# Reordering the first loads of a fused attention and gated-unit kernel: projection rows first, the first tile in halves on a second queue

## The chip, the cores and the metric

One core of a Trainium2 chip runs the whole program. The metric is device microseconds of one execution. The kernel before took 264.89 us, the median of three runs (264.78, 264.89, 264.89).

## The reference, cut to what matters

The input x has 2048 rows of 640 columns in bf16. It is normalised row by row, and the normalised rows feed two branches whose results are added to x:

```
xn  = (x - mean) / sqrt(var + 1e-5)                      # per row, no gain or bias
q, k, v = split(xn @ wqkv)                               # 640 -> 3 x 640, 32 heads of 20
A   = softmax(q . k[s - 2w], w = 0..7, masked) @ v[...]  # 8 keys per position, 2 apart
A   = A @ wo
B   = ((xn @ w_gate) * (xn @ w_up)) @ w_down             # 640 -> 1536 -> 640
out = x + A + B
```

Every product after the first step needs xn transposed (columns on partitions), so nothing of the real matrix work can start before one tile of 128 rows is loaded, normalised and transposed.

## The kernel before, in words

The work on x goes by 16 tiles of 128 rows (t = 0 to 15); the projections and the gated unit go by four blocks of 512 rows. Columns are handled in five chunks of 128, since a matmul contracts over 128 partitions.

An order is planned at build time by a small list scheduler in the kernel (class Sched). Each engine's work is yielded as tasks, with an estimated ready time; the scheduler keeps a clock for every engine (`K.t`) and emits the task that its estimates let start first, by priority. `land=` gives the scheduler the time at which a load is expected to land, and `occ=` the time that an operation is expected to take. These numbers only order the instructions: on the chip every engine runs its own list in that order, and semaphores make it wait for what it reads.

Per tile, `front(t)` makes this chain: the load of x (`x_load`, a DMA of 160 KB); two statistics instructions of 320 columns each on VectorE (L577); their aggregate (L580); a square root on ScalarE (L587); a reciprocal (L594); the normalisation into XNS on VectorE (L606 for tiles 0 and 1, in two parts of 256 and 384 columns; L609 for tiles 2 to 5); five transposes on TensorE (L645, `trans`) into PSUM for tiles 0 to 3; and copies from PSUM into XNT (ScalarE L658, VectorE L656 and L665). From tile 4 on the transpose is a DMA issued by SyncE (L678).

`proj_group` makes the Q and K products. For tiles 0 and 1 (`spread`, L733) the contraction is cut into steps given by `STEPS`, chunks 0 and 1, then 2, then 3 and 4, so that a step can start when its chunks are there. Q and K of tiles 0 and 1 are 100 matmuls of 128 columns. Later tiles use L701. The weights WQKV come by `wqkv_load(g, lo, hi)`: g = 0 is Q, 1 is K, 2 is V, and lo to hi are the chunks (rows of the weight matrix, 160 KB per chunk).

Before the first transposes TensorE has no data; `warm` gives it matmuls on constants (L685): ten of 512 columns from the start, and three of 256 columns behind tile 0's transposes.

All loads of the first stage go through SyncE's queue, in this order: x tile 0; Q chunks 0 to 2 (480 KB); x tile 1; K chunks 0 to 2 (480 KB); Q chunks 3 and 4 (320 KB); x tile 2; K chunks 3 and 4 (320 KB); x tiles 3 to 11; V (800 KB); x tiles 12 to 15, each of which waits for its buffer. ScalarE's queue carries one small read named `touch` (5 KB: 64 bytes from every eighth row of the Q columns, into a buffer TCH that nothing reads), issued at the same time as tile 0. ScalarE then loads its activation table (1.28 us) before its first square root.

The main part that follows is a stream of matmuls: projections (L701), logits (L1016), gate and up (L1318), the sums of the weighted values (L1254), down and output projection (L1419, L1470), while VectorE and GpSimd make the products of attention.

Of the kernel before, what the change touches and what calls it, by code (L numbers as in the profile page):

```python
# [11 lines left out]
NCH = 5  # L12
# [9 lines left out]
TS = 128  # L22
# [335 lines left out]
def build_kernel(nc, A_x, A_wqkv, A_wo, B_x, B_w_gate, B_w_up, B_w_down, out):  # L358
# [5 lines left out]
    def sb(name, shape, dtype=BF16, at=None):  # L364
        n = mybir.dt.size(dtype)
        for s in shape[1:]:
            n *= s
        n = (n + 63) // 64 * 64
        if at is None:
            at = place[0]  # L370
            place[0] += n
        assert at + n <= 229344, (name, at + n)
        return K.sbuf(name, shape, dtype, at)
# [65 lines left out]
    MV = sb("MV", [128, NT, 2], FP32)  # L439
    SD = sb("SD", [128, NT, 4], FP32)  # L440
    DUM = sb("DUM", [128, 16], FP32)
    TCH = sb("TCH", [128, NCH, 32])
    ZERO = sb("ZERO", [128, JB])
    UF = [sb("UF0", [128, JB], at=a_xr + 4 * D * 2), ZERO]
    EPSC = sb("EPSC", [128, 16], FP32)
# [17 lines left out]
    def mark(*k):  # L463
        done.add(k)
# [38 lines left out]

    PARTS = (((0, 2), (2, NCH)), ((0, 2), (2, NCH)))
    COPY = (("act", "act"), ("dve", "act"))
    STEPS = (((0, 2), (2, 3), (3, NCH)), ((0, 2), (2, 3), (3, NCH)))

    def part_of(t, c):
        return next(k for k, (lo, hi) in enumerate(PARTS[t]) if lo <= c < hi)

    def xslot(t):
        return t + 4 if t < 8 else t - 8

    def x_load(t, eng="sp", land=None):
        dma(XST[:, xslot(t), :], xhbm[t * TS:(t + 1) * TS, :], w=[XST[:, xslot(t), :]], name=f"xld{t}", eng=eng, land=land)
        mark("x", t)

    wqkv_src = A_wqkv.rearrange("(c p) n -> p c n", p=128)

# [49 lines left out]
    def front(t):  # L569
        x, st = XST[:, xslot(t), :], STATS[:, t, 0:12]  # L570
        xs, mv = XNS[:, t % NXN, :], MV[:, t, 0:2]
        sd, rstd, nmr = SD[:, t, 0:1], SD[:, t, 1:2], SD[:, t, 2:3]
        p = 0.1 * t

        def stats(i):
            o, a = st[:, 6 * i:6 * i + 6], x[:, i * DHALF:(i + 1) * DHALF]
            op("dve", lambda e: e.bn_stats(o, a), r=[a], w=[("st", t, i)], name=f"bn{t}_{i}", occ=0.49)  # L577

        def aggr():
            op("dve", lambda e: e.bn_aggr(mv, st), r=[("st", t, 0), ("st", t, 1)], w=[("mv", t)], name=f"bnag{t}", occ=0.2)  # L580

        ts = next((g for g in GROUPS if t in g), (t,))
        t0, t1 = ts[0], ts[-1] + 1

        def sqrt():
            o, i = SD[:, t0:t1, 0:1], MV[:, t0:t1, 1:2]
            op("act", lambda e: e.activation(o, i, ACT.Sqrt, bias=EPSC[:, 0:1]), r=[("mv", k) for k in ts] + [EPSC[:]],  # L587
               w=[("sd", k) for k in ts], name=f"sd{t}", occ=0.36)
            for k in ts:
                mark("sd", k)  # L590

        def recip():
            o, i = SD[:, t0:t1, 1:2], SD[:, t0:t1, 0:1]
            op("dve", lambda e: e.reciprocal(o, i), r=[("sd", k) for k in ts], w=[("rstd", k) for k in ts], name=f"rstd{t}", occ=0.16)  # L594
            if t >= N_DVE_A:
                n, m = SD[:, t0:t1, 2:3], MV[:, t0:t1, 0:1]
                op("dve", lambda e: e.scalar_tensor_tensor(n, m, -1.0, o, op0=ALU.mult, op1=ALU.mult),
                   r=[x for k in ts for x in (("mv", k), ("rstd", k))], w=[("nmr", k) for k in ts], name=f"nmr{t}", occ=0.13)
            for k in ts:
                mark("rstd", k)  # L600

        def apply():
            if t < N_SPLIT:
                for a, b in [(128 * lo, 128 * hi) for lo, hi in PARTS[t]]:
                    o, i = XNS[:, t, a:b], x[:, a:b]
                    op("dve", (lambda o, i: lambda e: e.tensor_scalar(o, i, mv[:, 0:1], rstd, op0=ALU.subtract, op1=ALU.mult))(o, i),  # L606
                       r=[i, ("mv", t), ("rstd", t)], w=[o], name=f"lnap{t}", occ=0.09 + (b - a) * 0.55e-3)
            elif t < N_DVE_A:
                op("dve", lambda e: e.tensor_scalar(xs, x, mv[:, 0:1], rstd, op0=ALU.subtract, op1=ALU.mult),  # L609
                   r=[x, ("mv", t), ("rstd", t)], w=[xs], name=f"lnap{t}", occ=0.45)  # L610
            else:
                op("act", lambda e: e.activation(xs, x, ACT.Identity, bias=nmr, scale=rstd),
                   r=[x, ("nmr", t), ("rstd", t)], w=[xs], name=f"lnap{t}", occ=0.75)
            mark("apply", t)

        yield have("x", t)
        if t == 1:
            yield have("apply", 0)
        for i in range(2):
            if t == 2 and i == 0:  # L620
                yield have("apply", 1)
            if t == 2 and i == 1:
                yield have("xnt", t - 1)
            if t in BN_AFTER and i == 1:
                yield have("rstd", t - 1)
            yield Task("dve", lambda: stats(i), r=[x], prio=p)
        yield Task("dve", aggr, r=[("st", t, 1)], prio=p)
        mark("mv", t)
        if t == ts[-1]:
            yield Task("act", sqrt, r=[("mv", t)], prio=p - 1)  # L630
            yield Task("dve", recip, r=[("sd", t)], prio=p)
        yield have("rstd", t)
        if t >= NXN:
            yield have("xnt", t - NXN)
        yield Task("dve" if t < N_DVE_A else "act", apply, r=[("rstd", t), x], w=[xs], prio=p)
        o = XNT[:, :, t * TS:(t + 1) * TS]
        if t < N_PE_T:
            hold = []

            def trans(*bs):  # L640
                tpvs = [PS[:, b, :].bitcast(BF16)[:, 0:NCH * 128].rearrange("p (c f) -> p c f", c=NCH) for b in bs]
                b, tpv = bs[0], tpvs[0]
                for c in range(NCH):
                    i, q = xs[:, c * 128:(c + 1) * 128], tpvs[part_of(t, c) if len(bs) > 1 else 0][:, c, :]
                    op("pe", (lambda q, i: lambda e: e.transpose(q, i, IDENT[:]))(q, i), r=[i, IDENT[:]], w=[q],  # L645
                       name=f"tr{t}_{c}", occ=0.057, lat=0.2)
                hold.extend(zip(bs, tpvs))
                if t == 0:
                    warm(3)

            def part(k, eng):
                b, tpv = hold[k]
                lo, hi = PARTS[t][k]
                a, i = o[:, lo:hi], tpv[:, lo:hi]
                if eng == "dve":
                    X = op("dve", lambda e: e.tensor_copy(a, i), r=[PS[:, b, :]], w=[a], name=f"xntcp{t}_0", occ=0.1 + 0.08 * (hi - lo))  # L656
                else:
                    X = op("act", lambda e: e.activation(a, i, ACT.Copy), r=[PS[:, b, :]], w=[a], name=f"xntcp{t}_1",  # L658
                           occ=0.12 + 0.12 * (hi - lo))
                K.free_bank(b, X)  # L660

            def copy():
                b, tpv = hold[0]
                if t < N_DVE_C:
                    X = op("dve", lambda e: e.tensor_copy(o, tpv), r=[tpv], w=[o], name=f"xntcp{t}", occ=0.49)  # L665
                else:
                    X = op("act", lambda e: e.activation(o, tpv, ACT.Copy), r=[tpv], w=[o], name=f"xntcp{t}", occ=0.75)
                K.free_bank(b, X)

            yield Task("pe", trans, r=[xs], prio=p, banks=len(PARTS[t]) if t < N_SPLIT else 1)  # L670
            if t < N_SPLIT:
                for k, e in enumerate(COPY[t]):
                    yield Task(e, (lambda k, e: lambda: part(k, e))(k, e), r=[PS[:, hold[k][0], :]], prio=p - 1)
            else:
                yield Task("dve" if t < N_DVE_C else "act", copy, r=[PS[:, hold[0][0], :]], prio=p)
        else:
            def dmat():
                op("sp", lambda e: e.dma_start_transpose(o, xs), r=[xs], w=[o], dma=True, name=f"dtr{t}", nbytes=200e3, occ=1.25, extra=1.3)  # L678

            yield Task("sp", dmat, r=[xs], prio=1)  # L680
        mark("xnt", t)
# [830 lines left out]
    N_DVE_A = 6  # L1512
    N_DVE_C = 5
    N_SPLIT = 2
    FIRST = 9
    GU_KEEP = 3
    HP_MAX = 0
# [3 lines left out]
    H_PRIO = 9  # L1521
    FIN_PRIO = 8

    x_load(0, land=3.2)
    tch = A_wqkv.rearrange("(c k p) n -> k c p n", k=16, c=NCH)[:, :, 0, 0:32]
    stores.append(dma(TCH[0:16], tch, w=[TCH[0:16]], name="touch", eng="act"))
    wqkv_load(0, 0, 3, land=5.1)
    x_load(1, land=5.5)
    wqkv_load(1, 0, 3, land=7.1)
    wqkv_load(0, 3, NCH, land=8.0)  # L1530
    x_load(2, land=8.5)
    wqkv_load(1, 3, NCH, land=9.6)
    K.t["act"] = 2.1
    warm(10, JB)

    def misc():
        yield have("xnt", NT - 1)
# [61 lines left out]
```

## Time and profile before

| what | value |
|---|---|
| median of 3 runs | 264.89 us |
| profiled execution, whole | 265.17 us |
| its span, first to last instruction | 263.4 us |
| TensorE busy in the span | 259.6 us (99%) |
| VectorE / ScalarE / GpSimd busy | 219.1 / 112.8 / 160.5 us |
| mean DMA rate over the span | 151 GB/s |
| DMA rate from 3 to 12 us, in the views of that stretch | 347 to 365 GB/s |
| granted TensorE clock | 1.0 throughout |

The span is the time from the first to the last instruction of one profiled execution; 1.77 us of that execution lie around it. Times in the timeline are counted from the start of the span. A matmul's end is modelled (a 128-column one is given 219 ns, though the next one starts some 57 ns later), so the spacing of starts is what tells the rate.

### The profile page before, as it was taken

How to read it: one execution, taken by the hardware profiler on the slowest of the kernel's cores; microseconds unless marked ns; L12 is line 12 of the kernel's file. 1: busy time of each engine (PE TensorE's matmuls, PEld its weight loads, DVE VectorE, ACT ScalarE, POOL GpSimd, SP SyncE). 2: the span in 40 equal slices, each digit the busy share in tenths (PEclk: the TensorE clock that was granted, in tenths of full speed). 3: DMA queues.
4: the chain of work that ended last, by engine and by line, in shares of the span. 5: the costliest groups of instructions: out<-in, count | busy, mean ns of one | idle time of the engine just before them, and what ended most of it. 6: DMA issues, size and time to landing. Idle time of an engine off the chain costs nothing.

```text
span 263.4 us, 4101 instructions
## 1 busy us (share of the span) xinstructions
PE 259.6 (99%) x1587; PEld 136.0 (52%) x1587; DVE 219.1 (83%) x259; ACT 112.8 (43%) x198; POOL 160.5 (61%) x97
## 2 busy tenths in 40 slices
PE   8999999999999999999999999999999999999996
PEld 3996964544444444444444444444444444445675
DVE  4798899999898798868779999999989989995041
ACT  3569987556622221224257665541324116211300
POOL 3000000000599999999983455899979999999300
PEclk9999999999999999999999999999999999999999
DMA  6985679933379996650249702566669865821621
GB/s 220 368 210 105 124 159 388 355 152 100 119 147 193 234 217 115 121 100 1 65 118 311 174 6 51 133 137 175 142 179 185 207 141 141 142 60 36 91 66 50
DMA packets 47843, 39.78 MB, mean 151 GB/s; under 512 B 23856, under 2 KB 45488, under 8 KB 47792
## 3 DMA queue, kind: packets, MB, share of 16 engines
q1 hardware_dynamic: 44848, 33.29, 48.4%
q0 software_dynamic: 2736, 6.16, 13.8%
q8 instruction: 12, 0.20, 0.3%
q10 hardware_dynamic: 240, 0.07, 0.1%
q14 instruction: 7, 0.06, 0.1%
HBM read 25.07 MB, written 7.23 MB: 123 GB/s over the span
## 4 chain that ended last, share of the span: by engine, by line
PE 96%; DMA 2%; SPq 0%; DVE 0%; issue 0%
PE PS L1318 39%; PE PS L701 23%; PE PS L1419 21%; PE PS L1470 7%; PE PS L1016 2%; DMA WQKV<-in_A_wqkv_dram 2%; PE PS L733 2%; PE PS L1254 2%; SPq L482 0%; PE PS L645 0%; DVE FB L1483 0%
## 5 line engine op out<-in xcount | busy, mean ns | idle before, releaser
L1200 POOL TENSOR_TENSOR SV<-PV 128x1024 bf16<-128x1024 f32 x40 | 94.1, 2524 | 17.8 <-DVE SM L1049 4.2
L1195 DVE TENSOR_TENSOR PV<-VX,PS 128x1024 f32<-128x1024 bf16 (+1 forms) x54 | 90.7, 1730 | 2.8 <-POOL SV L1200 2.8
L701 PE MATMUL PS<-XNT,WQKV 128*128 128x512 bf16 (+2 forms) x390 | 60.7, 316 | 0.0
L1318 PE MATMUL PS<-XNT,WG 128*128 128x512 bf16 x240 | 59.7, 379 | 0.0
L1318 PE MATMUL PS<-XNT,WU 128*128 128x512 bf16 x240 | 59.6, 379 | 0.0
L701 PEld LDWEIGHTS PS<-XNT,WQKV 128*128 128x128 bf16 x390 | 37.8, 112 | 21.9 <-ACT LOG L1027 0.8
L933 DVE TENSOR_TENSOR PRF<-PS,KT 128x1024 f32<-128x1024 f32 x32 | 38.0, 1218 | 0.3 <-PE PS L701 0.3
L1318 PEld LDWEIGHTS PS<-XNT,WG 128*128 128x128 bf16 x240 | 23.3, 98 | 28.7 <-issue 0.4
L1318 PEld LDWEIGHTS PS<-XNT,WU 128*128 128x128 bf16 x240 | 23.5, 98 | 28.3
L959 POOL TENSOR_TENSOR PRF<-PRF,PRF 128x1024 f32<-128x1024 f32 x8 | 21.0, 2634 | 21.6 <-DVE LOG L1076 21.6
L706 ACT ACTIVATE HT<-PS 128x512 bf16<-128x512 f32 x24 | 14.4, 598 | 35.4 <-PE PS L1318 35.4
L1419 PE MATMUL PS<-HT,WD 128*128 128x512 bf16 x120 | 27.5, 379 | 0.0
L884 DVE TENSOR_TENSOR PRD<-QT,KT 128x2048 bf16<-128x2048 bf16 x24 | 27.5, 1220 | 0.0
L706 ACT ACTIVATE UX<-PS 128x512 bf16<-128x512 f32 x15 | 9.0, 597 | 41.6 <-PE PS L1419 41.6
L1035 POOL MEMSET LOG<- 32x6 bf16 (+6 forms) x7 | 0.4, 95 | 42.8 <-ACT LOG L1027 42.8
L992 POOL TENSOR_TENSOR PRD<-PRF,PRF 128x1024 bf16<-128x1024 f32 x8 | 20.6, 2633 | 0.1
L970 POOL TENSOR_TENSOR PRF<-PRF,PRD 128x1024 f32<-128x1024 f32 x8 | 19.7, 2563 | 0.0
L1419 PEld LDWEIGHTS PS<-HT,WD 128*128 128x128 bf16 x120 | 11.7, 98 | 14.3 <-ACT OT L1263 0.4
L1419 PE MATMUL PS<-OT,WO 128*128 128x512 bf16 x75 | 18.6, 379 | 0.0
L1327 DVE TENSOR_TENSOR HT<-HT,PS 128x512 bf16<-128x512 bf16 x18 | 12.3, 686 | 7.2 <-PE PS L1318 7.1
L1483 DVE TENSOR_TENSOR FB<-PS,XR 128x320 bf16<-128x320 f32 (+2 forms) x9 | 4.1, 454 | 16.2 <-PE PS L1470 15.3
L577 DVE BATCH_NORM_STATS2 STATS<-XST 128x6 f32<-128x320 bf16 x32 | 14.2, 467 | 2.3 <-DMA XST<-in_A_x_dram 2.1
(76 smaller groups left out, 247.2 us busy)
## 6 DMA issues: line engine op xcount, KB each, us to landing
VX<-v_scratch SPq DMA_DIRECT2D x80, 130.0 KB, 3.0
PRF<-PRF POOLq DMA_DIRECT2D x8, 512.0 KB, 5.4
XST<-in_A_x_dram SPq DMA_DIRECT2D x16, 160.0 KB, 5.2
v_scratch<-VST SPq DMA_DIRECT2D x4, 640.0 KB, 6.4
WG<-in_B_w_gate_dram SPq DMA_DIRECT2D x1, 1920.0 KB, 8.8
WU<-in_B_w_up_dram SPq DMA_DIRECT2D x1, 1920.0 KB, 12.4
out_dram<-in_A_x_dram SPq DMA_DIRECT2D x1, 1920.0 KB, 18.1
WD<-in_B_w_down_dram SPq DMA_DIRECT2D x1, 1920.0 KB, 8.4
```

What stands on the lines that cost most here:

```text
L701: op("pe", (lambda o, l, x, c, first: lambda e: e.matmul(o, l, x, start=first, stop=(c == NCH - 1)))(o, l, x, c, first), r=[l, x], w=[o], ...
L706: X = op("act", (lambda o, i: lambda e: e.activation(o, i, ACT.Copy))(o, i), r=[i], w=[o], name=name, occ=0.12 + n * 0.9e-3)
L884: op("dve", lambda e: e.tensor_tensor(s[:], qb, kv, ALU.mult), r=[q, rk], w=[s[:]], name=f"prod{j}_{r}_{c}", occ=1.15, lock=True)
L933: X = op("dve", lambda e: e.tensor_tensor(o[:], qb, kv, ALU.mult), r=[q, rk, ("qev", j, c)], w=[o[:]], name=f"prow{j}_{r}_{c}_{q0}", occ=1.17)
L959: yield Task("pool", lambda: op("pool", lambda e: e.tensor_tensor(x, x, y, ALU.add), r=[x, y] + tokens(), w=[x], name=name, occ=2.36, lock ...
L970: yield Task("pool", lambda: op("pool", lambda e: e.tensor_tensor(x, x, z, ALU.add), r=[x, z] + tokens(), w=[x], name=name + "c", occ=2.36 ...
L992: yield Task("pool", lambda: op("pool", lambda e: e.tensor_tensor(o, a, y, ALU.add), r=[a, y] + tokens(), w=[o], name=f"qend{j}_{r}_{q0}", ...
L1195: last[0] = op("dve", lambda e: e.tensor_tensor(p, vw, a, ALU.mult), r=[vv] + rk, w=[p], name=f"pv{u}_{x}_{r0}", occ=0.09 + 1.1 * nr)
L1200: X = op("pool", lambda e: e.tensor_tensor(o, p[:, :, 0, :], p[:, :, 1, :], ALU.add), r=[p[:]] + tokens(), w=[o], name=f"pva{u}_{x}", occ= ...
L1318: op("pe", (lambda l, x, c: lambda e: e.matmul(PS[:, b, :], l, x, start=(c == 0), stop=(c == NCH - 1)))(l, x, c), r=[l, x], w=[PS[:, b, :] ...
L1419: op("pe", (lambda l, x, i: lambda e: e.matmul(PS[:, b, :], l, x, start=(i == 0), stop=(i == n - 1)))(l, x, i), r=[l, x], w=[PS[:, b, :]], ...
L1470: op("pe", (lambda l, x, i: lambda e: e.matmul(dst, l, x, start=(i == 0), stop=(i == n - 1)))(l, x, i), r=[l, x], w=[PS[:, b, :]], name=f" ...
```

## The change

- Loads on SyncE's queue now run: Q chunks 0 to 2; K chunks 0 and 1 (320 KB); Q chunks 3 and 4; x tile 2; K chunks 2 to 4 (480 KB); x tiles 3 to 11 and so on as before.
- x tile 0 is issued on ScalarE's queue, as two DMAs of 320 columns each (80 KB, rows of 640 bytes); x tile 1 follows on the same queue. Each statistics instruction of tile 0 waits for its own half only.
- The read `touch` and its buffer go.
- The steps of tile 0's projection become chunks 0 and 1, then 2, then 3, then 4. The transposes of tiles 0 and 1 become two tasks each (two chunks, three chunks) with a PSUM bank each, where one task had made all five.
- One warming matmul fewer at the start (nine).
- The landing times given to the scheduler, and ScalarE's starting clock, are new.

In the resulting order of TensorE's instructions, the part up to tile 2's transposes reads as follows (number of matmuls; `tr` are transposes, `c` chunks):

```
before: 10 warm | tr0 5 | 3 warm | Q0 c0-2 15 | K0 c0-1 10 | tr1 5 | Q0 c3-4 10 | Q1 c0-1 10 | Q1 c2-4 15, K0 c2 5 | K0 c3-4 10 | tr2
after:   9 warm | tr0 5 | 3 warm | Q0 c0-2 15 | K0 c0-1 10 | tr1 2 | Q0 c3 5 | tr1 3 | Q0 c4 5 | Q1 c0-1 10 | Q1 c2-4 15 | K0 c2-3 10 | tr2
```

Further on, one group of five 512-column matmuls (a V projection of the first block) moves from before the first products of tiles 4 and 5 to just before the first logits. VectorE's order is unchanged. On ScalarE two more DMA issues stand ahead of the table load, and some evictions between about 40 and 70 us change places.

```diff
-    TCH = sb("TCH", [128, NCH, 32])
...
-    STEPS = (((0, 2), (2, 3), (3, NCH)), ((0, 2), (2, 3), (3, NCH)))
-
-    def part_of(t, c):
-        return next(k for k, (lo, hi) in enumerate(PARTS[t]) if lo <= c < hi)
+    STEPS = (((0, 2), (2, 3), (3, 4), (4, NCH)), ((0, 2), (2, 3), (3, NCH)))
...
+    def x_half(i, land, eng="sp"):
+        c = slice(i * DHALF, (i + 1) * DHALF)
+        dma(XST[:, xslot(0), c], xhbm[0:TS, c], w=[XST[:, xslot(0), c]], name=f"xld0_{i}", eng=eng, land=land)
+        if i:
+            mark("x", 0)
...
-            yield Task("dve", lambda: stats(i), r=[x], prio=p)
+            yield Task("dve", lambda: stats(i), r=[x[:, i * DHALF:(i + 1) * DHALF]] if t == 0 else [x], prio=p)
...
-            def trans(*bs):
-                tpvs = [PS[:, b, :].bitcast(BF16)[:, 0:NCH * 128].rearrange("p (c f) -> p c f", c=NCH) for b in bs]
-                b, tpv = bs[0], tpvs[0]
-                for c in range(NCH):
-                    i, q = xs[:, c * 128:(c + 1) * 128], tpvs[part_of(t, c) if len(bs) > 1 else 0][:, c, :]
+            def trans(k, *bs):
+                hold.extend((b, PS[:, b, :].bitcast(BF16)[:, 0:NCH * 128].rearrange("p (c f) -> p c f", c=NCH)) for b in bs)
+                for c in range(*PARTS[t][k]) if t < N_SPLIT else range(NCH):
+                    i, q = xs[:, c * 128:(c + 1) * 128], hold[k][1][:, c, :]
...
-                hold.extend(zip(bs, tpvs))
-                if t == 0:
-                    warm(3)
+                if t == 0 and k:
+                    warm(N_WARM)
...
-            yield Task("pe", trans, r=[xs], prio=p, banks=len(PARTS[t]) if t < N_SPLIT else 1)
             if t < N_SPLIT:
-                for k, e in enumerate(COPY[t]):
+                for k, ((lo, hi), e) in enumerate(zip(PARTS[t], COPY[t])):
+                    yield Task("pe", (lambda k: lambda *bs: trans(k, *bs))(k), r=[xs[:, lo * 128:hi * 128]], prio=p, banks=1)
                     yield Task(e, (lambda k, e: lambda: part(k, e))(k, e), r=[PS[:, hold[k][0], :]], prio=p - 1)
             else:
+                yield Task("pe", lambda b: trans(0, b), r=[xs], prio=p, banks=1)
...
+    N_WARM = 3
...
-    x_load(0, land=3.2)
-    tch = A_wqkv.rearrange("(c k p) n -> k c p n", k=16, c=NCH)[:, :, 0, 0:32]
-    stores.append(dma(TCH[0:16], tch, w=[TCH[0:16]], name="touch", eng="act"))
-    wqkv_load(0, 0, 3, land=5.1)
-    x_load(1, land=5.5)
-    wqkv_load(1, 0, 3, land=7.1)
-    wqkv_load(0, 3, NCH, land=8.0)
-    x_load(2, land=8.5)
-    wqkv_load(1, 3, NCH, land=9.6)
-    K.t["act"] = 2.1
-    warm(10, JB)
+    wqkv_load(0, 0, 3, land=4.8)
+    x_half(0, 2.8, "act")
+    x_half(1, 3.2, "act")
+    x_load(1, eng="act", land=4.2)
+    wqkv_load(1, 0, 2, land=5.9)
+    wqkv_load(0, 3, NCH, land=6.8)
+    x_load(2, land=7.3)
+    wqkv_load(1, 2, NCH, land=8.6)
+    K.t["act"] = 3.4
+    warm(9, JB)
```

## Prediction

> **What bounds the kernel now.** I read the chain of waits first. After one DMA that ends at 7.40 us it is TensorE to the last piece, without a gap:
>
> ```profile
> 2.26 5.14 DMA WQKV<-in_A_wqkv_dram
> 7.40 0.05 issue
> 7.45 0.75 PE PS L733 x10
> 8.20 0.28 PE PS L645 x5
> 8.48 2.86 PE PS L733 x50
> ...
> 14.41 29.39 PE PS L701 x235
> ...
> 261.16 0.02 issue
> 261.19 0.29 DVE FB L1483
> ```
>
> The work of TensorE is fixed, so the end moves by what its start and the stalls ahead of about 14 us move, unless a new stall opens. Next I read the timeline of the first 25 us (start, duration):
>
> ```profile
> 3.36 0.89 DVE L577 BATCH_NORM_STATS2 STATS<-XST 128x6 f32<-128x320 bf16 x2 [2.12 <-DMA XST<-in_A_x_dram]
> 6.26 1.00 PE L733 MATMUL PS<-XNT,WQKV 128*128 128x128 bf16 x15
> 7.45 0.75 PE L733 MATMUL PS<-XNT,WQKV 128*128 128x128 bf16 x10 [0.19 <-DMA WQKV<-in_A_wqkv_dram]
> ...
> 8.52 0.49 ACT L658 ACTIVATE XNT<-PS 128x384 bf16<-128x384 bf16 x1 [1.46 <-PE PS L645]
> 9.14 0.70 ACT L706 ACTIVATE QT<-PS 128x640 bf16<-128x640 f32 x1
> 9.95 0.30 ACT L587 ACTIVATE SD<-MV,EPSC 128x1 f32<-128x1 f32 x1
> 10.48 0.45 DVE L609 TENSOR_SCALAR XNS<-XST,MV,SD 128x640 bf16<-128x640 bf16 x1
> 11.18 0.44 PE L645 MATMUL PS<-IDENT,XNS 128*128 128x128 bf16 x5
> ```
>
> The statistics of tile 0 start when it has landed (3.33); from there to the first product (6.26) is one chain over VectorE, ScalarE and TensorE. The fifteen products start 57 ns apart (the chain has fifty in 2.86), so the last began at 7.06 and the next was due at 7.11. It came at 7.45: the modelled ends show a gap of 0.19, the starts one of 0.34.
>
> Then the DMA issues (KB each, us to landing) and the rates by stretch (last two columns: busy share of the DMA engines, GB/s):
>
> ```profile
> XST<-in_A_x_dram SPq DMA_DIRECT2D x1, 160.0 KB, 2.5
> TCH<-in_A_wqkv_dram ACTq DMA_DIRECT2D x1, 5.0 KB, 2.3
> ```
>
> ```profile
> 2.25:2.75 0.50, 0.50 (x3) 0.15 (x1) 0.00 (x0) 0.29 (x1) 0.28 (x2) 1.00 1.15 312
> 2.75:3.25 0.50, 0.50 (x2) 0.15 (x1) 0.00 (x0) 0.00 (x0) 0.28 (x3) 1.00 0.65 103
> 3.25:5.25 2.00, 1.76 (x5) 0.44 (x3) 1.46 (x5) 0.30 (x1) 0.51 (x3) 1.00 1.05 373
> ```
>
> Outside the hole from 2.75 to 3.25 the engines are full: bytes put ahead of a tile delay it by 160 KB per 0.45 us.
>
> **The change, part by part.**
>
> *Tile 0 in halves beside Q (the disputed term).* What counts is when the second statistics instruction starts: 3.36 + 0.445 = 3.81 before. Afterwards it is the later of the second half's landing + 0.03 and the first's + 0.48. A landing at 3.78 changes nothing. No row shows two queues sharing the engines on bulk loads. The early end is the nearest lighter row on that queue, a 64 KB store from ScalarE's queue late in the kernel, 1.6 us to landing: the halves, issued at 0.83 and about 1.25, would land at 2.43 and 2.85, a gain of 0.9. The late end has all 480 KB of Q served first: 3.33 + 1.33 = 4.66, a loss of 0.9. I take TCH, the row nearest in queue, place and moment: the first half lands at 0.83 + 2.3 = 3.13, the second 0.42 later, 3.55, since the hole has room for Q's bytes. The second statistics then start at 3.61: gain 0.20.
>
> *K chunks 0 and 1 as 320 KB, ahead of tile 2.* 1120 KB stand up to its end instead of 1280, 0.45 us less, so about 6.95 instead of 7.40, and the products need it at 7.06 - 0.20 + 0.05 = 6.9: the 0.34 go. Q chunks 3 and 4 (1440 KB instead of 1600) land near 7.85 where they landed at 8.3. Five transposes took 0.31 at 8.04 where the chain gives 0.28; that 0.03 goes too. Gain 0.37, or 0.3 if either is late by a tenth.
>
> *New order before tile 2's transposes: a new wait.* Counted with tile 0 unmoved: 6.26, 15 products to 7.10, 10 to 7.69, two transposes to 7.80, five products to 8.09, three transposes to 8.26, five products to 8.55, then 35 at 57 ns to 10.53. Tile 2 must be normalised by then. ScalarE's copy of the three chunks (0.49) can start at 8.46, the eviction of Q (0.70) behind it ends at 9.67, and the square root of tile 2 is queued behind both: 9.69 instead of 9.95. From there to the normalised tile took 0.98 (9.95 to 10.93), so it is ready at 10.67 and the transposes start at 10.72: TensorE waits 0.20. If tile 2 lands no earlier than 8.76 the wait is 0.45; with 0.45 us fewer bytes ahead I don't expect that. Everything behind on TensorE waits with it.
>
> *One V group moved back.* Five 512-column matmuls, 5 x 0.216 = 1.08 us, no longer stand before the products of tiles 4 and 5. Those began at 24.09 (two matmuls after 23.65 in this row), and need tile 5's transposing DMA:
>
> ```profile
> 19.43 1.27 SPq L678 DMA_TRANSPOSE XNT<-XNS  x1
> ```
>
> ```profile
> XNT<-XNS SPq DMA_TRANSPOSE x1, 3.7
> ```
>
> ```profile
> 23.65 0.92 PE L701 MATMUL PS<-XNT,WQKV 128*128 128x512 bf16 x5
> ```
>
> It lands at 23.13; TensorE now arrives at 23.01, and with 0.05 from landing to start waits 0.17 (0 if the first transpose, 2.29 us of issue at 17.09, shortens like its followers of 1.2 to 1.28; 0.6 if it doesn't follow TensorE's earlier start). The group is done later, in a stretch that stays full.
>
> *Parts that cost nothing.* One warming matmul less: TensorE stood idle from the end of the warming at about 5.0 to 5.45. Two more issues on ScalarE (0.45 each) put its table load (1.28) at about 2.15 to 3.45; the first square root was at 4.52, so 0.9 us cover it even with tile 0 earlier by 0.2. SyncE has two issues fewer ahead of tile 3; its queue is a backlog of bytes, so nothing moves. Dropping TCH frees 5 KB. The split of tile 0's transposes keeps their order.
>
> Sum: -0.20 - 0.37 + 0.20 + 0.17 = -0.20. The profiled execution took 265.17 (span 263.4), 0.28 above the median 264.89; set against the median, **264.7 us**.
>
> **The rivals.** 0.2%, 0.53 us, is about what a measurement tells from no change here.
>
> *Faster: the halves keep ahead of Q.* Were each half over as fast as its smaller size allows, at 2.8 and 3.2, the second statistics start at 3.28, gain 0.53; if one of the two new waits also fails to open, 0.53 + 0.37 - 0.2 = 0.70: 264.2 us. For it: the hole shows engines idle just there. Against it: TCH, 5 KB, needed 2.3.
>
> *The same, from packet for packet.* If the engines take one row of Q (1280 bytes) for each half row of tile 0 (640), 320 KB of Q go ahead of the second half: 3.33 + 0.9 = 4.23, loss 0.45, all else as above: 265.35, within 0.2%. The Trainium skill ("DMA: Bandwidth & Descriptors", Queues, rings and completion order) says that each engine takes turns between queues packet by packet, and that DMAs from different engines end up interleaved on the same 16; by that rule a second queue gives tile 0 no precedence. The trace of before bears on it only by TCH, whose packets ran in the same stretch as tile 0's.
>
> *Slower: Q first.* If Q's 480 KB, issued at the same moment and without the small read ahead of them, hold the engines, the second half lands at 4.66: loss 0.89, less the other terms' zero balance: 265.8 us. From a landing of 4.3 on it is slower by over 0.2%. For it: the hole is Q's own first packets being slow. Against it: it needs a whole queue to be passed over.
>
> *Slower: the changed order of Q chunk 3.* Three transposes of tile 1 now stand behind five products that wait for Q chunks 3 and 4. Should those land at 8.31 as before, the transposes move from 8.10 to 8.63 and all behind them by 0.53: 265.2; half a microsecond later still, 265.7.
>
> *Slower: the clock.* The warming matmuls start 0.43 apart until 4.22 and 0.40 apart after it, so the rate rises within the ninth, which is now the last. If it slipped to the end of an equally long busy stretch (3.75 us from 5.3), some forty matmuls would take 57 ns more: +2.3, 267. The Trainium skill ("TensorE: Matmul & The Clock Gate", Part 1) calls the window free-running and the moment variable from run to run; three runs within 0.11 us show none of that.
>
> **How the numbers follow.** My forecast 0.32, packet for packet 0.08, halves ahead 0.31, Q first 0.19, Q chunk 3 late 0.05, the clock 0.05. So faster 0.31, same 0.40, slower 0.29. The likeliest case alone: 264.4 to 265.1. The range reaches below the faster rival by 0.2 (both waits smaller) and to Q first: 264.0 to 265.8.
>
> **What would show it.** Right: statistics of tile 0 start separately near 3.2 and 3.6; the first L733 near 6.06; no DMA named before the K products; L645 of tile 2 waiting for XNS some 0.2; a DMA wait ahead of the first 256-column L701 of tiles 4 and 5. Wrong: a second statistics instruction before 3.3 or after 4.2, a wait for WQKV inside the first 40 products, or any TensorE idle beyond 25 us.

## The result: 1.2% slower

The changed kernel takes 267.99 us, the median of five runs (267.68 to 268.88), against 264.89 for the kernel before in the same comparison (264.78 to 264.98): a ratio of 1.0123, 95% interval 1.0112 to 1.0134. The forecast was 264.7 with a range of 264.0 to 265.8. The sign and the range were both wrong.

The profiled execution took 268.88 us with a span of 267.1 (before: 263.4), so it is 0.89 above its own median; its terms below are sized on it and are a little too large for the median. It also differs from the four others in its mean granted clock, listed as 1.000 where they have 0.994; the last section says what that means.

The chain of waits of the changed kernel (start, length, what) now hangs on tile 0's second half; `...` stands for lines left out:

```profile
0.83 0.43 ACTq L481
1.26 0.03 issue
1.29 4.13 DMA XST<-in_A_x_dram
5.42 0.02 issue
5.44 0.50 DVE STATS L579
...
7.14 0.79 PE PS L646 x5
7.93 0.64 PE PS L686 x3
8.57 2.67 PE PS L734 x25
11.23 0.21 PE PS L646 x2
11.45 0.53 PE PS L734 x5
11.98 0.32 PE PS L646 x3
12.30 2.44 PE PS L734 x40
14.74 0.28 PE PS L646 x5
...
18.09 29.39 PE PS L702 x235
```

The chain of before has, for tile 2's transposes and the 25 products behind them:

```profile
11.34 0.28 PE PS L645 x5
11.62 1.40 PE PS L733 x25
```

Three things are to be seen. The second half lands at 5.42 us, issued at 0.83 + 0.43. Tile 0's transposes start at 7.14, where they started at 5.45 before: 1.69 us. And 25 products take 2.67 us where 25 took 1.40 before. From there on nothing is new: the stream of 235 begins at 18.09 instead of 14.41 and takes 29.39 us in both, and the last piece of TensorE's work ends 3.7 us later as well.

The timeline has the two statistics instructions of tile 0 apart, as the change meant them to be, but late:

```profile
3.93 0.49 DVE L579 BATCH_NORM_STATS2 STATS<-XST 128x6 f32<-128x320 bf16 x1 [2.69 <-DMA XST<-in_A_x_dram]
5.44 0.49 DVE L579 BATCH_NORM_STATS2 STATS<-XST 128x6 f32<-128x320 bf16 x1 [1.02 <-DMA XST<-in_A_x_dram]
7.14 0.79 PE L646 MATMUL PS<-IDENT,XNS 128*128 128x128 bf16 x5 [2.28 <-DVE XNS L608]
7.72 0.85 PE L686 MATMUL PS<-const-bfloat16-1.0 128*128 128x256 bf16 x3
```

and before:

```profile
5.45 0.63 PE L645 MATMUL PS<-IDENT,XNS 128*128 128x128 bf16 x5 [0.45 <-DVE XNS L606]
5.92 0.50 PE L685 MATMUL PS<-const-bfloat16-1.0 128*128 128x256 bf16 x3
```

Before, the statistics ran back to back from 3.36, the second from 3.81. TensorE stood idle for 2.28 us ahead of the transposes, 0.45 before.

**Where the 3.7 us of span went.** 1.69 are the later transposes. From tile 0's transposes to those of tile 2 it was 5.89 us before (5.45 to 11.34 in the chain) and is 7.60 now (7.14 to 14.74), although five products fewer stand between them (5 x 57 ns = 0.28, which come behind instead: 3.35 from tile 2's transposes to the stream of 235, where it was 3.07). So for equal work this stretch costs 1.99 more. Rows of the chain account for it: the three warming matmuls take 0.64 where 0.33 is their length at full rate, the first 25 products 1.27 more, the rest up to 14.74 about 0.7 more, tile 0's five transposes 0.1 more (0.58 from their start to that of the warming matmuls behind them, 0.47 before); that is 2.4, and the 0.34 that TensorE waited for K's rows before is gone, which leaves 2.0.

The cause of the long products is the rate of TensorE, and the profile's page hides it. The busy time by stretch (PE busy and number of matmuls first, then the other engines; the last three columns are granted clock, DMA share and GB/s), before:

```profile
9.60:12.60 3.00, 3.00 (x58) 3.00 (x56) 2.20 (x8) 1.95 (x4) 0.00 (x0) 1.00 1.07 362
```

and after:

```profile
7.10:9.60 2.50, 2.46 (x20) 2.12 (x21) 2.07 (x7) 1.15 (x3) 0.00 (x0) 1.00 1.07 363
9.60:12.60 3.00, 3.00 (x31) 3.00 (x29) 1.08 (x4) 0.26 (x1) 0.00 (x0) 1.00 1.07 363
12.60:15.00 2.40, 2.40 (x46) 2.40 (x44) 1.22 (x4) 1.81 (x4) 0.00 (x0) 1.00 1.07 362
```

TensorE is fully busy in both, and the column of the granted clock says 1.00 in both, but it does 31 matmuls in the 3 us where it did 58. Only the count, or the spacing of starts (107 ns up to 12.5 us, 57 ns after 12.6), shows half rate. In the trace's own record the first stretch at full rate begins at 4.60 us before and at 12.61 us after.

### The profile page after: what moved, and what is told of

It is laid out like the page before. It is cut to its first block, busy times and chain, and to the rows that moved or that the text cites. A ratio compares the mean times of both kernels' runs of the same rounds, so it can differ in the third digit from the quotient of the medians.

```text
span 267.1 us, 4099 instructions
## 1 busy us (share of the span) xinstructions
PE 261.7 (98%) x1586; PEld 138.1 (52%) x1586; DVE 218.9 (82%) x259; ACT 112.6 (42%) x198; POOL 160.5 (60%) x97
## 4 chain that ended last, share of the span: by engine, by line
PE 96%; DMA 2%; DVE 1%; ACTq 0%; ACT 0%; issue 0%
PE PS L1319 39%; PE PS L702 22%; PE PS L1420 21%; PE PS L1471 7%; PE PS L734 3%; PE PS L1017 2%; PE PS L1255 2%; DMA XST<-in_A_x_dram 2%; PE PS L646 1%; PE PS L686 0%; DVE STATS L579 0%; ACTq L481 0%; DVE XNS L608 0%; ACT SD L589 0%; DVE FB L1484 0%
```

## The experiments

Twelve kernels were run, each beside the kernel before, whose median was 264.94 to 265.08 in these comparisons. In the code, too, `...` stands for lines left out. The theory after the result: the DMA engines served all of Q (480 KB) between tile 0's two halves, and the idle stretch that this made cost TensorE its rate.

**1. Why the second half came late.** Three edits of the changed kernel: all loads on SyncE's queue, with the halves ahead of Q (`one_queue`); Q's load cut in three (`q_chunks`); tile 0 as one load on ScalarE's queue, both statistics waiting for all of it (`x0_whole`).

```diff
 one_queue
-    wqkv_load(0, 0, 3, land=4.8)
-    x_half(0, 2.8, "act")
-    x_half(1, 3.2, "act")
-    x_load(1, eng="act", land=4.2)
+    x_half(0, 2.8)
+    x_half(1, 3.2)
+    wqkv_load(0, 0, 3, land=4.8)
+    x_load(1, land=4.2)
 q_chunks
-    wqkv_load(0, 0, 3, land=4.8)
+    for c in range(3):
+        wqkv_load(0, c, c + 1, land=4.8)
 x0_whole
-    x_half(0, 2.8, "act")
-    x_half(1, 3.2, "act")
+    x_load(0, eng="act", land=2.8)
...
-            yield Task("dve", lambda: stats(i), r=[x[:, i * DHALF:(i + 1) * DHALF]] if t == 0 else [x], prio=p)
+            yield Task("dve", lambda: stats(i), r=[x], prio=p)
```

> The changed kernel with every load on SyncE's queue, in the order: the two halves of tile 0, Q chunks 0 to 2, tile 1, K chunks 0 and 1, Q chunks 3 and 4, tile 2, K chunks 2 to 4. All instructions of the other engines are as in the changed kernel, nine warming matmuls too, and the touching read stays away. Theory (it is the second queue that makes the second half late): the halves land at 3.1 and 3.4, the second statistics start near 3.6, TensorE idles under 0.8 us and runs at full rate; 264.9 - 0.2 - 0.37 + 0.37 = 264.7 us (264.3 to 265.2). Rival (the loss comes from the missing touching read, from nine warming matmuls or from the new order of TensorE's instructions): 266 us or more.

> The changed kernel with Q chunks 0 to 2 loaded by three DMAs of 160 KB in a row where one of 480 KB stood; the halves of tile 0 stay on ScalarE's queue. Theory (the DMA engines take turns between the two queues by whole DMAs: first half, all of Q, second half, K, tile 1): now only 160 KB stand between the halves, 320 KB fewer, 0.9 us, so the second half lands at about 4.5 instead of 5.41, and the time falls by 0.9 if the half-rate stretch moves along: 267.1 us (266.3 to 267.5), 265 to 266 if the shorter idle time keeps the rate up. Rival (turns by rows or bytes, or the first queue simply has precedence): second half at 5.2 to 5.6, 267.7 to 268.9 us.

> The changed kernel with tile 0 as one DMA of 160 KB on ScalarE's queue instead of two halves; all else is unchanged. Theory (turns by whole DMAs): tile 0 is served whole in the first turn and lands at 3.9 + 0.45 = 4.3, both statistics run from there, so the second starts at 4.8 instead of 5.44: 0.65 us less, 267.3 us (266.6 to 267.7), less still if the rate rises earlier. Rival (turns by rows or bytes, or precedence of the first queue): the whole tile lands at about 5.4, the second statistics start at 5.9, 268.5 us (268.1 to 269.3).

Measured: `one_queue` 265.43 us (ratio 1.0039, 1.0009 to 1.0068; ten of its twelve runs lie between 265.23 and 266.82, two at 269, which were not profiled and list a granted clock of 0.994 where the ten have 1.000); `q_chunks` 266.97 (1.0073, 1.0059 to 1.0088); `x0_whole` 267.23 (1.0073, 1.0051 to 1.0094). The start of tile 0's statistics in the timelines, in this order:

```profile
2.73 1.08 DVE L579 BATCH_NORM_STATS2 STATS<-XST 128x6 f32<-128x320 bf16 x2 [1.50 <-DMA XST<-in_A_x_dram]
```

```profile
3.71 1.03 DVE L579 BATCH_NORM_STATS2 STATS<-XST 128x6 f32<-128x320 bf16 x2 [2.47 <-DMA XST<-in_A_x_dram]
```

```profile
3.98 0.89 DVE L579 BATCH_NORM_STATS2 STATS<-XST 128x6 f32<-128x320 bf16 x2 [2.74 <-DMA XST<-in_A_x_dram]
```

On one queue, ahead of Q, both halves are worked through by 3.81, and with that nearly all of the loss is gone. The median of 265.43 is still above the range of the theory (265.2) and below that of its rival; in its trace tile 1 lands at 6.20, where it was 5.39 before. `q_chunks` and `x0_whole` came out in the ranges of their theory. On two queues the landings of the trace tell how the turns go. In the changed kernel: first half 3.90, Q 5.19, second half 5.42, K's 320 KB 6.37, tile 1 6.83. With Q in three: Q's first 160 KB 3.51, first half 3.69, Q's second 4.04, second half 4.23, Q's third 6.11, tile 1 6.31, K 7.31. So the two queues go as if they took turns by whole loads, for loads of 80 to 480 KB: behind its first load, a load on the second queue waits for one load of the first queue, and with 480 KB in that load it waits for 480 KB. In `x0_whole` the single 160 KB need only one turn and are there at 3.96, before Q (5.15).

One rival is left open: that the engines serve the loads of both queues in the order of their issue. The issues go side by side, some 0.45 us apart on each queue (in the changed kernel at 0.82, 1.33 and 1.86 on SyncE's, at 0.83, 1.29 and 1.77 on ScalarE's), so both rules give the same landings, or differ only where two issues stand within 25 ns; no run separates them. By either rule the second half waits for all of Q, and less when Q is cut.

The prediction weighed a turn of one row for one row; none of the three runs agrees with that. The Trainium skill ("DMA: Bandwidth & Descriptors", Queues, rings and completion order) has the engines change queues at packet boundaries, a packet being 9 to 17 descriptors as a rule and 64 at most. By that rule a turn can be as long as an engine's share of Q (384 rows of 1280 bytes over 16 engines, 24 rows), and the landings do not speak against it; the rule that the prediction took from that section, row for row, was a misreading of what a packet is.

**2. What half rate costs, and what brings it on.** The changed kernel with four or nine more warming matmuls behind its nine (`warm13`, `warm18`); the kernel before with nine or four instead of ten (`before_warm9`, `before_warm4`); the order of all other work stays.

```diff
 warm18 (warm13: 4 instead of 9)
...
     warm(9, JB)
+    more_warm(9)
 before_warm9 (before_warm4: 4 instead of 9, 6 * 0.427)
-    warm(10, JB)
+    warm(9, JB)
+    K.t["pe"] += 0.427
```

`more_warm` issues the same 512-column matmuls as `warm`; the last line keeps the scheduler's clock, and with it the order of the other instructions, where it was.

> The changed kernel with eighteen warming matmuls of 512 columns instead of nine, so that TensorE is busy until about 6.5 us and idle for some 0.6 us instead of 2.5 before tile 0's transposes. Theory (the loss has two parts: tile 0's second half is late, 5.41 instead of 3.78 at most, and TensorE then stands idle and runs at half rate, 107 ns per 128-column matmul, until 12.6): the first transposes stay at about 7.1, the matmuls behind them start 57 ns apart, and the half-rate part goes. It is 7.44 (7.14 to 14.58) less 5.27 worked out for full rate = 2.2 us of the profiled 268.88; so about 266.0 us (265.6 to 266.7) against the 267.99 median. Rival (the half rate costs nothing, because the products would wait for something else anyway): 267.7 to 268.9, unchanged.

> The kernel before with nine warming matmuls instead of ten, nothing else. Theory (the length of TensorE's idle stretch decides the half rate, not the number of warming matmuls): the nine end near 4.85 and tile 0's transposes still start at 5.45, an idle stretch of 0.6 us, far below the 1.35 to 2.3 us of the runs that went to half rate. No change: 264.9 to 265.2 us, projection matmuls at 57 ns. Rival (the tenth matmul is what carried the full rate over): half rate to about 12.6 us as in the changed kernel, 266.5 to 267.5 us.

> The kernel before with four warming matmuls instead of ten, nothing else: every load as before, but TensorE idle from about 2.6 to 5.45 us. Theory (half rate is a cost of its own, which a long idle stretch ahead of tile 0's transposes brings on): matmuls of 128 columns 107 ns apart from 5.45 until a whole stretch of some 3.4 us has been busy, so until 9 to 12 us; half of that time lost less the 0.34 us that TensorE waited for K's rows anyway: 266.2 to 267.6 us. Rival (the loads set the pace of this stretch and hide a slower TensorE): 265.0 to 265.5 us.

> The changed kernel with thirteen warming matmuls instead of nine, which end between 5.7 and 6.6 us, so that none stands in the way of tile 0's transposes near 7.1 (eighteen ended at 7.33). Theory (the loss is the late second half, some 1.7 us, less about 0.3 saved later, plus the half rate, and the half rate goes with the idle stretch): full rate by 7.1 in the profiled run, 266.2 to 266.7 us, below the eighteen's 266.96. Rival (only a TensorE kept busy to the very transposes keeps the rate): 267.4 to 268.5 us.

Measured: `warm18` 266.96 us (1.0070, 1.0056 to 1.0085); `warm13` 266.67 (1.0088, 1.0056 to 1.0120); `before_warm9` 265.10 (1.0000, 0.9992 to 1.0009); `before_warm4` 266.76 (1.0062, 1.0043 to 1.0081). From the chain of `warm13`:

```profile
1.29 3.91 DMA XST<-in_A_x_dram
...
6.92 0.28 PE PS L646 x2
...
7.89 1.40 PE PS L734 x25
```

The second half is as late as in the changed kernel (5.20), but 25 products take 1.40 us: full rate. That run took 266.23. From the chain of `before_warm4`, where the loads are those of the kernel before:

```profile
5.39 0.79 PE PS L645 x5
6.19 0.64 PE PS L685 x3
6.83 2.25 PE PS L733 x25
9.08 0.28 PE PS L645 x5
```

Tile 0 is on time (5.39), and the 25 products take 2.25 us. So each of the two costs something by itself. The late half alone (`warm13`) costs 1.7 us by the medians and 1.1 in the profiled run (266.23 against 265.17); a long idle stretch alone (`before_warm4`) costs 1.8 by the medians and 0.8 in the profiled run (265.97). In the changed kernel they come together and make 3.1, or 3.7 in the profiled run. These figures do not add up exactly: the four runs of either experiment spread over 1.3 us or more, and the time at which the rate rises differs from trace to trace (8.49 us in `before_warm4`, 12.61 in the changed kernel).

The rival "the loads hide a slower TensorE" fell, and so did "only an unbroken TensorE keeps the rate" (`warm13` stood idle for 0.36 us ahead of its transposes and kept it). But four more warming matmuls do not keep the rate in every execution: one of the four runs of `warm13`, 268.81, lists a granted clock of 0.994. One warming matmul less costs nothing where tile 0 is on time. `warm18` came out between its two ranges. It ends its warming at 7.33 in its chain, behind the time at which `warm13` has begun its transposes (6.92), though tile 0 is normalised at about the same time in both (from 6.55 and 6.52), so part of it is in the way.

**3. The parts alone.** The kernel before without the touching read (`before_no_touch`), and with K's first load cut to 320 KB and the steps of tile 0's projection cut to match (`before_k320`).

```diff
 before_no_touch
-    tch = A_wqkv.rearrange("(c k p) n -> k c p n", k=16, c=NCH)[:, :, 0, 0:32]
-    stores.append(dma(TCH[0:16], tch, w=[TCH[0:16]], name="touch", eng="act"))
 before_k320
-    wqkv_load(1, 0, 3, land=7.1)
-    wqkv_load(0, 3, NCH, land=8.0)
-    x_load(2, land=8.5)
-    wqkv_load(1, 3, NCH, land=9.6)
+    wqkv_load(1, 0, 2, land=6.6)
+    wqkv_load(0, 3, NCH, land=7.5)
+    x_load(2, land=8.0)
+    wqkv_load(1, 2, NCH, land=9.3)
...
-    STEPS = (((0, 2), (2, 3), (3, NCH)), ((0, 2), (2, 3), (3, NCH)))
+    STEPS = (((0, 2), (2, 3), (3, 4), (4, NCH)), ((0, 2), (2, 3), (3, NCH)))
```

> The kernel before without the touching read, nothing else. Theory A (the first read of the weights is slow and the touching read takes that on itself): Q and all that stands behind it on SP's queue come 0.3 to 0.8 us later, TensorE's wait for K's rows at 7.45 us grows by as much: 265.2 to 265.8 us. Theory B (the touching read was free and useless): 264.9 to 265.1 us, K's rows awaited to 7.45 as before.

> The kernel before with K's first load cut from 480 to 320 KB and its last raised to match, the steps of the first tile cut accordingly; tile 0 whole, touching read and ten warming matmuls stay. Theory (the prediction's term for K's rows stands when taken alone): the wait for K at 7.45 us goes or shrinks and tile 1's transposes move from 8.04 to 7.7 to 7.9: 264.6 us (264.4 to 264.9). Rival (the next load takes the wait over, so that the split gives nothing): 265.0 to 265.4 us.

Measured: 265.01 us (1.0000, 0.9992 to 1.0009) and 264.99 us (0.9998, 0.9989 to 1.0006). Neither part moves the time. The chain of `before_no_touch`, which still has K's 480 KB, has no wait for K's rows:

```profile
0.86 4.43 PE PS L685 x10
5.28 0.79 PE PS L645 x5
6.08 0.62 PE PS L685 x3
6.70 1.40 PE PS L733 x25
8.10 0.28 PE PS L645 x5
8.38 2.79 PE PS L733 x50
```

The rate rose later here (the three matmuls of 256 columns still take 0.62), so the products began later, and K's rows had landed by 6.91, not 7.40: the 25 ran through without a wait, and tile 1's transposes came at 8.10, where the profile before had 8.20. `before_warm9` has the same K load too, and there the rows land at 7.71 and the wait is longer than before:

```profile
7.76 0.75 PE L733 MATMUL PS<-XNT,WQKV 128*128 128x128 bf16 x10 [0.55 <-DMA WQKV<-in_A_wqkv_dram]
```

The profiled runs follow it: 264.99 us without the wait, 265.17 with K at 7.40, 265.47 with K at 7.71, while the medians of these kernels are the same. `before_k320` had no wait for K in its trace either and took 264.88. So the wait differs from one execution to the next, and I had taken the wait of one execution for one of the kernel. How many executions have it is not known, since one of each kernel was traced.

**4. Is there a faster order?** Tile 0's halves on two queues, the first ahead of Q, the second ahead of the touching read, K's 320 KB, ten warming matmuls (`split_start`); the same with tile 1 ahead of Q (`x1_first`); and the changed kernel with only the first half moved ahead of Q, Q in three, ten warming matmuls (`turns`).

```diff
 split_start
+    TCH = sb("TCH", [128, NCH, 32])
...
-    wqkv_load(0, 0, 3, land=4.8)
-    x_half(0, 2.8, "act")
+    x_half(0, 2.8)
     x_half(1, 3.2, "act")
-    x_load(1, eng="act", land=4.2)
+    tch = A_wqkv.rearrange("(c k p) n -> k c p n", k=16, c=NCH)[:, :, 0, 0:32]
+    stores.append(dma(TCH[0:16], tch, w=[TCH[0:16]], name="touch", eng="act"))
+    wqkv_load(0, 0, 3, land=4.8)
+    x_load(1, land=4.2)
...
-    warm(9, JB)
+    warm(10, JB)
 x1_first, against split_start
-    wqkv_load(0, 0, 3, land=4.8)
     x_load(1, land=4.2)
+    wqkv_load(0, 0, 3, land=4.8)
 turns, against the changed kernel
-    wqkv_load(0, 0, 3, land=4.8)
-    x_half(0, 2.8, "act")
+    x_half(0, 2.8)
     x_half(1, 3.2, "act")
+    for c in range(3):
+        wqkv_load(0, c, c + 1, land=4.8)
...
-    warm(9, JB)
+    warm(10, JB)
```

> Tile 0's halves on two queues, the first ahead of Q on SP's and the second first on the scalar queue, the touching read behind it, Q, tile 1 and the rest on SP's, K's first load 320 KB, ten warming matmuls. Theory (the changed kernel loses only by Q being served ahead of the second half and by the idle stretch that follows): both halves are there by 3.0 us, tile 0's transposes start near 5.0 (5.45 before), no half rate, tile 1's statistics not later than 5.6: 264.5 us (264.2 to 264.9). Rival (the halves or the weights behind them come later again, and tile 1 or K's rows take over what tile 0 gains): 265.0 to 265.8 us.

> The kernel with tile 0's halves on two queues ahead of Q (split_start) with tile 1 issued ahead of Q instead of behind it, nothing else. Theory (there tile 1's landing at 5.94 us took back what tile 0 had gained): tile 1 lands by 4.5, its statistics start when VectorE is free at 5.3 instead of 5.96, tile 1's transposes near 7.45 instead of 8.06; Q lands near 5.95, just in time for the first product at 5.9 to 6.0: 264.4 us (264.2 to 264.7). Rival (the weights set the pace of this stretch, so whatever tile 1 gains is waited for at Q's or K's rows): 264.9 to 265.3 us.

> The changed kernel with the first half moved ahead of Q on SP's queue, Q in three loads of 160 KB, ten warming matmuls; the second half and tile 1 stay on ScalarE's queue. Theory (the queues take turns by whole loads, so that tile 1 on the second queue passes all but one of Q's loads): both halves by 3.1 us, tile 1 by 4.6 and Q by 5.6, tile 0's transposes near 5.1, the first product near 5.9, tile 1's transposes near 7.5 (8.06 with tile 1 behind Q on one queue); 264.6 us (264.3 to 264.9). Rival (the sooner start is waited for again at the next weights, as when tile 1 was issued ahead of Q): first product or K's rows later by as much, 264.9 to 265.5 us.

Measured: `split_start` 264.94 us (0.9998, 0.9987 to 1.0009), `x1_first` 265.44 (1.0018, 1.0006 to 1.0030), `turns` 265.44 (1.0016, 1.0007 to 1.0025). All three start tile 0's transposes sooner than before, near 5.1, and none is faster; the last two are slower by 0.2%. The timelines say what took it back, `split_start` first:

```profile
5.08 0.63 PE L647 MATMUL PS<-IDENT,XNS 128*128 128x128 bf16 x5 [0.61 <-DVE XNS L609]
5.96 0.89 DVE L580 BATCH_NORM_STATS2 STATS<-XST 128x6 f32<-128x320 bf16 x2 [0.65 <-DMA XST<-in_A_x_dram]
8.06 0.29 PE L647 MATMUL PS<-IDENT,XNS 128*128 128x128 bf16 x2 [0.45 <-DVE XNS L609]
```

then `x1_first`:

```profile
5.29 0.88 DVE L580 BATCH_NORM_STATS2 STATS<-XST 128x6 f32<-128x320 bf16 x2
7.00 1.73 PE L735 MATMUL PS<-XNT,WQKV 128*128 128x128 bf16 x25 [0.43 <-DMA WQKV<-in_A_wqkv_dram]
```

and `turns`:

```profile
5.11 0.63 PE L646 MATMUL PS<-IDENT,XNS 128*128 128x128 bf16 x5 [0.40 <-DVE XNS L608]
5.26 0.88 DVE L579 BATCH_NORM_STATS2 STATS<-XST 128x6 f32<-128x320 bf16 x2
5.91 1.00 PE L734 MATMUL PS<-XNT,WQKV 128*128 128x128 bf16 x15
7.34 0.75 PE L734 MATMUL PS<-XNT,WQKV 128*128 128x128 bf16 x10 [0.43 <-DMA WQKV<-in_A_wqkv_dram]
```

With tile 1 behind Q, its statistics wait for it (0.65 us). With tile 1 in time, the wait is for Q's rows, or for K's. In `turns` the loads landed in the order expected (Q's first load 4.20, tile 1 4.41, Q's second 4.82), and TensorE still waited 0.43 for K. So what arrives sooner in this stretch is waited for again at something else, as the rivals written for the last two said (the median of `x1_first` is 0.14 above its rival's range; that of `split_start` lies just above its theory's). It is not a mere exchange at one rate of bytes, though: the same 800 KB (tile 0, Q's 480 KB and tile 1) had landed by 5.39 us before, and by 5.94, 6.27 and 6.86 in these three traces. In `turns` and `x1_first` a slow stretch among the first loads, shown in the last section, makes most of that difference.

## Why the prediction was wrong, by its own steps

- *The term of tile 0 in halves* failed, and it decides the sign. I took the touching read's row (landing 2.3 us after its issue) for the first half's, and put the second half 0.42 behind it: 3.55. Measured, 3.90 and 5.42, with Q landing between them at 5.19; the second statistics start at 5.44 instead of 3.61, so the step that said "gain 0.20" lost 1.63 against the 3.81 before. A 5 KB read that shares its moment only with tile 0 says nothing on a load that shares it with 480 KB.
- *The late end of that term* was too early too. I put it at 4.66, by adding Q's time at the full rate to tile 0's old landing. Measured, 5.42. In the profile after, the engines moved 32 GB/s from 1.75 to 2.75 us, while before the slow half microsecond (103 GB/s, 2.75 to 3.25) came when most of tile 0's bytes had been moved. So the range would not have held the time even had the clock stayed: all four runs of `warm13` (266.23 and more) lie above 265.8.
- *The rival "Q first"* is the mechanism that happened, with 0.19, and its effect was mis-sized: 0.89 for the second half, measured 1.63.
- *The rival "the clock"* happened too, for the reason that the first one did. I gave it 0.05 and let it stand by itself, as an accident of the ninth warming matmul. It is a consequence: the later tile 0, the longer TensorE idles, the likelier is half rate. Its size, 2.3, took 57 ns more for each of forty matmuls; half rate adds 50 (107 less 57), which makes 2.0, and 1.99 was measured. Adding 2.3 to "Q first" (265.8) gives 268.1, near the 267.99 measured, but by luck: one term was too large and the other too small.
- *One warming matmul less costs nothing* holds by itself (`before_warm9`). The cover that I named, TensorE idle until 5.45, was the wrong question: I did not say what a longer idle stretch would do.
- *K chunks as 320 KB, gain 0.37*: not there in the median (`before_k320`, 0.9998). The wait was real in the profiled execution, and that was 0.28 above the median; in other traces with K's 480 KB it is absent (`before_no_touch`) or longer (`before_warm9`).
- *Tile 2's new wait, 0.20*: not seen. In the changed kernel TensorE was at half rate and came at 14.58 to a tile normalised at 14.39. In `split_start`, at full rate, no gap stands in the chain either, since tile 1 was later there than I counted.
- *Tile 5's transposing DMA, 0.17*: not seen; the stream of 235 matmuls across that point takes 29.39 us before and after.
- The expectations for the order of the instructions, for a shift of the end by what the start shifts, and for no new stall beyond 25 us held.

## What to carry to other kernels

A load on a second queue does not overtake a large load that was issued on the first ahead of it: here whole loads were served one after the other, so what must come first belongs ahead on the same queue, or the large load must be cut. When a term of a sum delays the first real work of TensorE, ask in the same line what the idle time does to its rate, and join the two rivals. And before costing a wait of a few tenths, ask whether it belongs to the kernel or to the one execution that was profiled.

## What the runs showed of the hardware

- *The rate of TensorE changes in steps of 3.41 us.* Eleven of the fourteen traces hold a record of it. In them the first full-rate stretch begins at 3.98 to 6.56 us where the warming runs up to the transposes or nearly, at 8.49 (`before_warm4`), 9.56 (`q_chunks`), 10.29 (`x0_whole`) and 12.61 (after) where it doesn't, and it is always 256.00 or 259.41 us long, lengths 3.41 apart. Counting back in such steps from 12.61 in the changed kernel, 5.79 to 9.20 has TensorE idle until 7.14, and only 9.20 to 12.61 is busy throughout: the rate rises at the end of the first busy window. The Trainium skill ("TensorE: Matmul & The Clock Gate", Part 1) describes such a window, free-running, of 3413 ns; the lengths above agree with it, as 75 and 76 windows. How busy a window must be is bounded only: 0.05 to 3.46 in `x0_whole`, busy from 0.86 (76%), was not enough, and 5.08 to 8.49 in `before_warm4`, busy from 5.39 (91%), was.
- *A granted clock of 0.994 is half rate of another kind.* Four of the five runs of the changed kernel list it, and so do the two runs of `one_queue` at 269, one of `x0_whole` (267.82) and one of `warm13` (268.81). The column does not count half rate ahead of the first full-rate stretch, for the profiled run of the changed kernel has 1.000 with half rate until 12.61. This points to full rate reached and lost again in the others, for some 3.2 us (an estimate: 2 x 0.006 x 266), about one such step. Of the changed kernel, then, the one execution that was profiled is not like the rest: there TensorE first came to full rate at 12.61. None of the runs at 0.994 was profiled, so when they lost the rate, and why two of `one_queue` did, stays open.
- *The first loads have a slow stretch, and it moves.* By stretch (columns as above), in `x1_first`:

```profile
2.25:3.25 1.00, 1.00 (x4) 0.29 (x2) 0.21 (x1) 0.78 (x1) 0.57 (x4) 1.00 1.07 315
3.25:4.25 1.00, 1.00 (x4) 0.32 (x3) 0.89 (x3) 0.04 (x1) 0.53 (x3) 1.00 0.67 93
```

and in `turns`:

```profile
3.25:4.50 1.25, 1.25 (x5) 0.40 (x3) 0.86 (x3) 0.29 (x1) 0.52 (x3) 1.00 1.08 361
4.50:5.75 1.25, 0.84 (x8) 0.46 (x8) 1.21 (x5) 0.32 (x1) 0.00 (x0) 1.00 0.83 182
```

In each of the traces whose rates were read, some half to one and a half microseconds of the first six pass at 30 to 180 GB/s, at another place by the order of the loads. With or without the touching read the time is the same (`before_no_touch`). What makes the stretch slow was not tried and stays open.
